# Row E of a Fourier-mixing kernel in four column tiles of TensorE, with another order of loads and weight conversions

## The chip, the cores and the metric

The kernel runs on one core of a Trainium2 chip. The metric is the device time of one execution in microseconds; the time before is the median of three runs. TensorE is PE in the profile, VectorE DVE, ScalarE ACT, GpSimd POOL, and SyncE, which here only starts transfers, SP.

## What is computed

```python
# x: (8, 3008, 256) f32; gate, val: (256, 1536); out: (1536, 256)
X = np.fft.fft(np.fft.fft(x, axis=1), axis=2).real   # (8, 3008, 256)
t = X.reshape(24064, 256)
gate = 1 / (1 + np.exp(-(t @ w_gate)))
return (gate * (t @ w_val)) @ w_out
```

The three weight matrices arrive as 64-bit floats and become 32-bit floats on the chip.

## The kernel before

Every batch is handled in two parts. First the transform along the 3008 positions: the rows of x are folded on each other by symmetry (`fold_ops`), so that 756 rows of 126 partitions times six remain, and matrices of cosines and sines (`st`, table 0 and 1) turn them into rows P (cosines), Q (sines) and E (cosines of the one feature in the middle, column `HD`), each for 1505 frequencies `k`. P and Q are 128 features wide and are named `pk` and `qk`. E is one row for each batch, but it is needed on all 128 partitions, as `ek`. Each row is made in two column blocks (even and odd frequencies, 377 and 376 columns), each block by six matmuls into two PSUM banks, `ev` and `od` (`half`); ACT copies `ev` to SBUF as `a`, and DVE places the sum and the difference of the two (`places`).

The transform along the features is merged into the weights: `merge` multiplies a piece of w_gate or w_val by the small table `dt` on PE (tile `ps`), ACT copies the result to `G1` and `G2`, and two small transfers spread one row of G2 over the partitions as `ge`, the factors of E.

The second part is the main loop. A step `i` is one half of a pair (batch, chunk of 256 frequencies, two blocks of 128 of the 1536 features). `front` makes four matmuls, `pa` from P and `pb` from Q; DVE adds E times `ge` to `pa` (`ae`, L364), and sum and difference with `pb` (`z`, L367 and L368); ACT takes the sigmoid (L575); `gate` multiplies (`h`, L379) and makes sums on POOL (`sf`). `back`, two pairs later, multiplies by the prepared forms `wf` of w_out (tile `po`). `finish` combines and stores. There are 576 steps.

Before any of it can run, the weights have to be converted, in 18 pieces, the `jobs`, each of gate (w = 0), val (1) or out (2), for column block c. `weight_load` brings one in on SP's queue, `weight_parts` is two operations on ACT (L172, L173), `weight_join` three on DVE (L182, L183, L185) and an add on POOL (L187). `weight_use` then merges a gate or val piece, or makes the forms of an out piece (POOL and ACT).

The order on every engine is the order in which the program is written (a manual schedule); waits follow from buffers. `side` and `pre` hold what is done beside a step: `at(i, f)` puts f after step i. [...] four rotate under the tag "x" (`psx`, for ps, pa, pb, ev, od), four belong to the output sums (`pso`). All transfers share eight semaphores in turn, so a transfer can wait for the one before it on its semaphore, and SP's queue waits with it.

Before, the loads start with two weight pieces, then x of batch 0, the cosines in two halves, four weight pieces, the sines in one transfer, and four more. Row E of batch 0 is made on all 128 partitions at once, with the middle column of x broadcast over 128 weight columns:

```python
W[b, blk] = (v[:, :, 0:HD], r[:, :, 0:HD],
             v[:, :, HD : HD + 1].to_broadcast([NP, NQ, P]))
```

The seven other rows E are made together in the main loop, at steps 40 and 42 (`e_rows`, seven weight columns), written to DRAM (`ed`) and read back for each batch onto 128 partitions by `seq_start`.

Of the kernel before, what the change touches and what calls it, by code (L numbers as in the profile page):

```python
# [45 lines left out]
def kernel(  # L46
# [66 lines left out]
    ge = const.tile([P, 2, NFT], F32, name="ge")  # L113

    x8 = const.tile([NP, B - 1, 4, NQ], F32, name="x8")
    ed = dram.tile([B - 1, NK], F32, name="ed")

    def load_table(t, nq):
        for q in range(0, NQ, nq):
            nc.sync.dma_start(out=st[:, t, q : q + nq], in_=stab[:, t, q : q + nq])  # L120

    jobs = [(w, c - (w == 2)) for c in range(NPR + 1) for w in range(3)
            if (c if w == 2 else c < NPR)]
    RAW, WS = {}, {}
    shared = {}
    KEEP = 10

    def weight_load(j):  # L130


        w, c = jobs[j]
        src = (moe_w_gate, moe_w_val, moe_w_out)[w]
        src = src[2 * c * P : 2 * (c + 1) * P, :] if w == 2 else src[:, c * WC : (c + 1) * WC]
        src = src.rearrange("(c p) f -> p c f", p=P)

        def some(n, pool, tag):

            key = tag, (j - 6) // 3 if tag == "c7" else 0  # L140
            if key not in shared:
                shared[key] = pool.tile([P, n, 2 * WC], F32, name=f"w{tag}", tag=tag)
            return shared[key]

        if j < KEEP:
            pool, tag = ((zp, "z"), (pqp, ("pk", "qk", "ek")[j % 3]), (op, "os"), (sp, "sf"))[
                j // 3 if j < 6 else j // 2 - 1]
            raw = pool.tile([P, 2, WC, 2], I32, name="raw", tag=tag)
            if j < 6:
                pool, tag = ((app, "ae"), (hp, "h"))[j // 3]  # L150
                ws = pool.tile([P, 2, WC], F32, name="ws", tag=tag)
            else:
                ws = some(3, cp, "c7")[:, (j - 6) % 3].rearrange("p (c f) -> p c f", c=2)
# [12 lines left out]

    def weight_parts(j):

        if j in RAW:
            raw, ws = RAW[j], WS[j]  # L170
            lo, hi = raw[:, :, :, 0], raw[:, :, :, 1]
            nc.scalar.activation(ws, hi.bitcast(F32), AF.Abs)  # L172
            nc.scalar.activation(lo, lo.bitcast(U32), AF.Copy, scale=2.0 ** -29)  # L173

    def weight_join(j):
        if j not in RAW:
            return
# [4 lines left out]
        ts(out=ws, in0=ws, scalar1=2.0 ** -15, scalar2=HUGE, op0=ALU.max, op1=ALU.min)  # L182
        ts(out=wi, in0=wi, scalar1=3, scalar2=0x3FFFFFF8, op0=ALU.logical_shift_left,  # L183
           op1=ALU.bitwise_and)
        nc.vector.scalar_tensor_tensor(out=wi, in0=hi, scalar=-(2 ** 30), in1=wi,  # L185
                                       op0=ALU.bitwise_and, op1=ALU.bitwise_or)
        nc.gpsimd.tensor_tensor(wi, wi, lo, op=ALU.add)  # L187
# [36 lines left out]
    def fold_ops(b, nq):  # L224
# [60 lines left out]
    def half(w, d, blk, sn, rows, other=None):  # L285


        c0, n = ((0, NE), (NE, NO))[blk]
        ev, od = [bank(name, other and other[i])[0:rows, 0:n] for i, name in enumerate(("ev", "od"))]

        def sums(*qs):
            for q in sorted(qs, key=lambda q: q % 2):
                mm((ev, od)[q % 2], w(q), st[:, int(sn), q, c0 : c0 + n], q < 2, q >= NQ - 2)

        def then():
            a = evp.tile([P, NE], F32, name="a", tag="a")[0:rows, 0:n]
            nc.scalar.copy(a, ev)
            return lambda: places(a)

        def places(a):  # L300
            nc.vector.tensor_tensor(d[:, blk : blk + 2 * n - 1 : 2], a, od, op=ALU.add)
            lo, hi = (od, a) if sn else (a, od)
            top = M - blk
            nc.vector.tensor_tensor(d[:, top : top - 2 * NO + 1 : -2], lo[:, 0:NO], hi[:, 0:NO],
                                    op=ALU.subtract)
        return sums, then

    def whole(sums, then):
        sums(*range(NQ))
        return then()  # L310

    def seq_start(b):
        PQE[b] = (pqp.tile([P, NK], F32, name="pk", tag="pk"),
                  pqp.tile([P, NK], F32, name="qk", tag="qk"),
                  pqp.tile([P, NK], F32, name="ek", tag="ek"))
        if b:
            nc.sync.dma_start(out=PQE[b][2], in_=ed[b - 1 : b, :].to_broadcast([P, NK]))

    def seq_group(b, blk, what, other=None):
        return half(lambda q: W[b, blk][what][:, q, :], PQE[b][what], blk, what == 1, P, other)  # L320


    ER = []

    def e_load():
        for b in range(1, B):
# [14 lines left out]
    def e_out():  # L341
        nc.scalar.dma_start(out=ed, in_=ER.pop())


    chunks = [(k0, min(CH, NK - k0)) for k0 in range(0, NK, CH)]
# [135 lines left out]


    nc.scalar.dma_start(out=dt, in_=dtab.rearrange("(c p) d -> p c d", p=P))
    for j in range(2):
        weight_load(j)
    load_x(0)
# [12 lines left out]
    weight_parts(0)  # L499
    weight_parts(1)  # L500
    weight_join(0)
    weight_join(1)
    weight_use(0)
    weight_use(1)
# [3 lines left out]
    for i, f in enumerate(fold_ops(0, NQ // 2)):  # L508
        f()
        for sums, _ in cos:  # L510
            sums(*range(i * NQ // 2, (i + 1) * NQ // 2))
    sin = [seq_group(0, blk, 1) for blk in range(2)]
    for sums, _ in sin:
        sums(*range(NQ))
# [6 lines left out]
    weight_use(2)  # L521

    per = 2 * NPR * len(chunks)
    side = {}
# [8 lines left out]


    pre = {}
    for j in range(9, len(jobs)):
        pre.setdefault(j - 9, []).append(lambda j=j: weight_parts(j))
        at(j - 9, lambda j=j: weight_join(j))
        if KEEP <= j < len(jobs) - 3:
            at(j - 9, lambda j=j: weight_load(j + 3))  # L540
# [97 lines left out]
```

## Time and profile before

| | |
|---|---|
| time, median of 3 (lowest to highest) | 2029.07 us (2028.25 to 2029.18) |
| span of the profiled execution | 2028.5 us, mean granted TensorE clock 0.996 |
| first P, E matmul / first Q matmul / first front | 23.85 / 43.84 / 54.92 us |
| last output matmul ends, by the chain | 2021.1 us |
| rows E of batches 1 to 7 | 200.63 to 204.53 and 211.21 to 215.10 us |

The page has one line for each engine with its busy time, its share of the span and its instructions. A 32-bit matmul stands in it as two records (the count of PE is twice the number of matmuls in the code), and the duration of a record is longer than the distance to the next, since matmuls overlap; the distance is what counts: 0.216 us for 256 columns, 0.317 us for 377. In a timeline each row is a start, a duration, engine and line, the operation, the result and its operand, and how many records follow each other; in square brackets is how long the engine was idle and what released it. A list of waits has the engine, its line and tile, what it waited for, the total in us, how often, and the longest.

### The profile page before, as it was taken

Reading aid. Unit: us, or ns where it says so; the run is one execution under the profiler, and the core shown is the slowest. Engines: PE = TensorE matmul, PEld = TensorE weight load, DVE = VectorE, ACT = ScalarE, POOL = GpSimd, SP = SyncE. Lnnn points to the kernel's source line nnn. Section 1 sums busy time; section 2 is a strip of 40 time slices with the busy share of each in tenths; the row PEclk is TensorE's granted clock in tenths of the full one; section 3 lists DMA queues with packets and bytes.
Section 4 is the critical chain, followed back from the end, with each engine's and each line's share of the span. In section 5 each row is a group of like instructions: output and inputs, shape, how many; then the busy total and the mean of one; then the engine's idle time right before and its main releaser. Section 6 shows DMA issues by size and latency. Waiting matters only on the chain.

```text
span 2028.5 us, 27347 instructions
## 1 busy us (share of the span) xinstructions
PE 1996.6 (98%) x9168; PEld 1743.3 (86%) x9168; DVE 1754.9 (87%) x3221; ACT 498.5 (25%) x875; POOL 1328.4 (65%) x1675
## 2 busy tenths in 40 slices
PE   5999999999999999999999999999999999999998
PEld 3788789888998889888898888988889888898888
DVE  6899778987899878997889977999879988898887
ACT  3422222222222222222222222222222222222222
POOL 3679555875569755696457955589446875565655
PEclk8999999999999999999999999999999999999999
DMA  8240002100021000200010000201002010000001
GB/s 260 84 74 11 27 11 74 33 12 11 11 81 27 11 11 17 76 26 11 16 60 28 27 16 16 73 10 37 11 11 72 16 31 11 11 16 16 11 16 26
DMA packets 136176, 70.98 MB, mean 35 GB/s; under 512 B 127875, under 2 KB 128131, under 8 KB 133642
## 3 DMA queue, kind: packets, MB, share of 16 engines
q1 hardware_dynamic: 134214, 68.69, 12.6%
q8 instruction: 74, 1.21, 0.3%
q10 hardware_dynamic: 1822, 0.54, 0.1%
q14 instruction: 66, 0.54, 0.1%
HBM read 44.50 MB, written 24.68 MB: 34 GB/s over the span
## 4 chain that ended last, share of the span: by engine, by line
PE 85%; DVE 7%; POOL 4%; DMA 2%; issue 1%; ACT 0%; DVEq 0%; SPq 0%; ACTq 0%; POOLq 0%
PE po L93 37%; PE pa L93 21%; PE pb L93 21%; PE ev L93 3%; PE od L93 3%; DVE ae L364 2%; DVE h L379 2%; DVE z L368 1%; DMA ge<-G 1%; DVE z L367 1%; POOL x L239 1%; POOL x L237 1%; DMA st<-in_stab_dram 1%; POOL sf L384 1%; POOL sf L383 1%
## 5 line engine op out<-in xcount | busy, mean ns | idle before, releaser
L575 ACT ACTIVATE z<-z 128x512 f32<-128x512 f32 (+1 forms) x576 | 358.5, 622 | 1319.1 <-DVE z L368 1319.1
L364 DVE SCALAR_TENSOR_TENSOR ae<-ek,ge,pa 128x256 f32<-128x256 f32 (+1 forms) x1152 | 489.7, 466 | 186.1 <-PE pa L93 181.9
L93 PE MATMUL pb<-qk,G 128*128 128x256 f32 (+1 forms) x2304 | 582.2, 375 | 2.5 <-DVE ae L364 2.5
L93 PE MATMUL pa<-pk,G 128*128 128x256 f32 (+1 forms) x2304 | 581.9, 375 | 0.0
L93 PE MATMUL po<-sf,wf 128*128 128x256 f32 (+1 forms) x2304 | 537.3, 376 | 1.0 <-POOL sf L384 0.2
L93 PEld LDWEIGHTS pa<-pk,G 128*128 128x128 f32 x2304 | 438.5, 190 | 55.9 <-issue 1.3
L93 PEld LDWEIGHTS po<-sf,wf 128*128 128x128 f32 x2304 | 437.2, 190 | 54.8 <-POOL sf L385 4.5
L93 PEld LDWEIGHTS pb<-qk,G 128*128 128x128 f32 x2304 | 438.2, 190 | 52.8 <-DVE ae L364 4.1
L383 POOL TENSOR_TENSOR sf<-h 128x256 f32<-128x256 f32 (+1 forms) x288 | 213.4, 741 | 386.9 <-DVE h L379 386.9
L379 DVE TENSOR_TENSOR h<-z 128x512 f32<-128x512 f32 (+1 forms) x576 | 454.7, 789 | 0.0
L367 DVE TENSOR_TENSOR z<-ae,pb 128x512 f32<-128x512 f32 (+1 forms) x576 | 390.1, 677 | 61.4 <-DVE ae L364 1.4
L93 PE MATMUL po<-h,wf 128*128 128x256 f32 (+1 forms) x1728 | 412.7, 375 | 0.0
L368 DVE TENSOR_TENSOR z<-ae,pb 128x512 f32<-128x512 f32 (+1 forms) x576 | 386.4, 671 | 0.0
L93 PEld LDWEIGHTS po<-h,wf 128*128 128x128 f32 x1728 | 329.1, 191 | 36.4
L381 POOL TENSOR_TENSOR sf<-h 128x256 f32<-128x256 f32 (+1 forms) x288 | 219.1, 761 | 210.0 <-DVE h L379 206.2
L384 POOL TENSOR_TENSOR sf<-sf,h 128x256 f32<-128x256 f32 (+1 forms) x288 | 215.4, 748 | 22.6
L385 POOL TENSOR_TENSOR sf<-h,sf 128x256 f32<-128x256 f32 (+1 forms) x288 | 214.0, 743 | 22.6
L466 ACT COPY c<-po 128x512 f32<-128x512 f32 (+1 forms) x141 | 76.7, 580 | 62.0 <-PE po L93 62.0
L93 PE MATMUL ev<-st,x 126*128 126x377 f32 (+3 forms) x216 | 78.0, 495 | 11.7 <-DMA st<-in_stab_dram 11.7
L426 DVE STREAM_TRANSPOSE os<-c 128x256 f32<-128x256 f32 x192 | 83.9, 437 | 0.2
L93 PE MATMUL od<-st,x 126*128 126x377 f32 (+3 forms) x216 | 75.3, 481 | 0.0
L471 POOL TENSOR_TENSOR c<-c 128x512 f32<-128x512 f32 (+1 forms) x47 | 73.5, 1565 | 0.0
(82 smaller groups left out, 711.4 us busy)
## 6 DMA issues: line engine op xcount, KB each, us to landing
x<-in_xf_dram SPq DMA_DIRECT2D x16, 1512.0 KB
out_dram<-os SPq DMA_DIRECT2D x288, 64.0 KB
ek<-ed SPq DMA_DIRECT2D x7, 752.5 KB
out_dram<-os SPq DMA_DIRECT2D x92, 56.0 KB
st<-in_stab_dram SPq DMA_DIRECT2D x2, 1111.9 KB
st<-in_stab_dram SPq DMA_DIRECT2D x1, 2223.7 KB
raw<-in_moe_w_gate_dram SPq DMA_DIRECT2D x4, 512.0 KB
raw<-in_moe_w_val_dram SPq DMA_DIRECT2D x4, 512.0 KB
```

Of the source, the lines that this page charges most:

```text
L93: nc.tensor.matmul(o, l, r, start=start, stop=stop, skip_group_check=True)
L364: nc.vector.scalar_tensor_tensor(out=ae[:, g], in0=ek[:, ks], scalar=ge[:, g, f : f + 1], in1=pa[:, g], op0=ALU.mult, op1=ALU.add)
L367: nc.vector.tensor_tensor(z[:, :, 0], ae, pb, op=ALU.add)
L368: nc.vector.tensor_tensor(z[:, :, 1, ::-1], ae, pb, op=ALU.subtract)
L379: nc.vector.tensor_tensor(h[:, fh], z[:, 0], z[:, 1], op=ALU.mult)
L381: tt(s[:, 2], h[:, 0, 0], h[:, 0, 1], op=ALU.subtract)
L383: tt(s[:, 0], h[:, 0, 1], h[:, 1, 1], op=ALU.add)
L384: tt(s[:, 1], s[:, 0], h[:, 0, 0], op=ALU.subtract)
L385: tt(s[:, 3], h[:, 1, 0], s[:, 1], op=ALU.subtract)
L426: nc.vector.transpose(os_[:, s, 0:nb, h, :], t[:, slot, 0 : nb * TB])
L466: nc.scalar.copy(t[:, 2 * j : 2 * j + 2, 0:n], PO[j][:, :, 0:n])
L575: nc.scalar.activation(z[:, 0], z[:, 0], AF.Sigmoid)
```

## The change

Row E of every batch is now made with one weight column for each row (one for batch 0, seven for the others). The four sums that a row needs (even or odd block, even or odd part) lie at partitions 0, 32, 64 and 96 of one PSUM bank, `pe`, that is in four column tiles of PE, and the matmuls go through the four in turn. ACT copies three of them out, DVE places the rows, and the result goes through DRAM to all partitions: for batch 0 as well, at the start, on ACT's queue. x and the cosines are loaded first, the sines in two halves, and only eight weight pieces ahead of the main loop. The conversion of the out pieces comes two pairs later in the order of the jobs, six pieces are converted ahead of the loop in place of nine, and `evacuate` has row E first. It is meant to take matmul time off PE and to let the transform start before the weights are in.

```diff
-    jobs = [(w, c - (w == 2)) for c in range(NPR + 1) for w in range(3)
-            if (c if w == 2 else c < NPR)]
+    jobs = [(w, c - 2 * (w == 2)) for c in range(NPR + 2) for w in range(3)
+            if (c >= 2 if w == 2 else c < NPR)]
-    KEEP = 10
+    KEEP = 8
...
-            W[b, blk] = (v[:, :, 0:HD], r[:, :, 0:HD],
-                         v[:, :, HD : HD + 1].to_broadcast([NP, NQ, P]))
+            W[b, blk] = (v[:, :, 0:HD], r[:, :, 0:HD], v[:, :, HD : HD + 1])
...
-    def e_rows(blk):
-        if not blk:
-            ER.append(cp.tile([B - 1, NK], F32, name="er", tag="c7"))
-        return whole(*half(lambda q: x8[:, :, 1 + 2 * blk, q], ER[0], blk, False, B - 1))
+    def e_sums(col, b, m, other=None):
+        ps = bank("pe", other)
+        tb = lambda blk, par: (2 * blk + par) * TB
+
+        def sums(*qs):
+            for n in range(max(sum(q % 2 == par for q in qs) for par in range(2))):
+                for blk in range(2):
+                    c0, k = ((0, NE), (NE, NO))[blk]
+                    for par in range(2):
+                        for q in [q for q in qs if q % 2 == par][n : n + 1]:
+                            t = tb(blk, par)
+                            mm(ps[t : t + m, 0:k], col(blk, q), st[:, 0, q, c0 : c0 + k],
+                               q < 2, q >= NQ - 2)
+
+        def then():
+            er = cp.tile([P, NK], F32, name="er", tag="c7")[0:m]
+            ev = evp.tile([P, NE], F32, name="a", tag="a")[0:m]
+            e1 = evp.tile([P, NE], F32, name="a", tag="a")[0:m]
+            nc.scalar.copy(ev, ps[tb(0, 1) : tb(0, 1) + m, 0:NE])
+            nc.scalar.copy(e1[:, 0:NO], ps[tb(1, 0) : tb(1, 0) + m, 0:NO])
+            return lambda: (places(er, 0, True, ev, ps[0:m, 0:NE]),
+                            last(er, ev, e1[:, 0:NO]))
+
+        def last(er, a, ev):
+            nc.scalar.copy(a[:, 0:NO], ps[tb(1, 1) : tb(1, 1) + m, 0:NO])
+            places(er, 1, False, ev, a[:, 0:NO])
+            nc.scalar.dma_start(out=ed[b : b + m], in_=er)
+
+    def e_spread(b):
+        (nc.sync if b else nc.scalar).dma_start(
+            out=PQE[b][2], in_=ed[b : b + 1, :].to_broadcast([P, NK]))
...
-    for j in range(2):
-        weight_load(j)
     load_x(0)
-    load_table(0, NQ // 2)
-    for j in range(2, 6):
-        weight_load(j)
-    load_table(1, NQ)
-    for j in range(6, KEEP):
+    load_table(0, 0)
+    load_table(0, NQ // 2)
+    load_table(1, 0)
+    for j in range(2):
+        weight_load(j)
+    load_table(1, NQ // 2)
+    for j in range(2, KEEP):
         weight_load(j)
...
-    cos = [seq_group(0, blk, what, (2 * blk, 2 * blk + 1) if what else None)
-           for blk in range(2) for what in (0, 2)]
+    first_e = e_sums(lambda blk, q: W[0, blk][2][:, q, :], 0, 1, 0)
+    cos = [first_e] + [seq_group(0, blk, 0) for blk in range(2)]
...
-    for then, js in zip(evacuate, ((2, 3, 4), (5,), (), (), (6, 7), (8,))):
+    for then, js in zip(evacuate, ((), (), (0,), (1, 2, 3), (4,))):
         weight_round(*js)
         then()()
+        if then is first_e[1]:
+            e_spread(0)
+    weight_round(5)
+    for j in range(3):
+        weight_use(j)
...
-    for j in range(9, len(jobs)):
-        pre.setdefault(j - 9, []).append(lambda j=j: weight_parts(j))
-        at(j - 9, lambda j=j: weight_join(j))
+    for j in range(6, len(jobs)):
+        i = j - 6 - (j > 12)
+        pre.setdefault(i, []).append(lambda j=j: weight_parts(j))
+        at(i, lambda j=j: weight_join(j))
...
-        at(2 * c + (-3, -2, 1)[w], lambda j=j: weight_use(j))
+        at((2 * c - 3, 2 * c - 2, min(2 * c + 3, j - 5))[w], lambda j=j: weight_use(j))
...
-    split(i0 + 28, e_rows, 0)
-    split(i0 + 30, e_rows, 1)
-    at(i0 + 32, e_out)
+    split(i0 + 30, lambda: whole(*e_sums(lambda blk, q: x8[:, :, 1 + 2 * blk, q], 1, B - 1)))
```

More of the change, by code (lines that the diff above doesn't have):

```diff
@@ L115, with load_table @@
     x8 = const.tile([NP, B - 1, 4, NQ], F32, name="x8")
[L116 to L120, printed above, removed]
-    jobs = [(w, c - (w == 2)) for c in range(NPR + 1) for w in range(3)
-            if (c if w == 2 else c < NPR)]
+    ed = dram.tile([B, NK], F32, name="ed")
+    def load_table(t, q):
+        nc.sync.dma_start(out=st[:, t, q : q + NQ // 2], in_=stab[:, t, q : q + NQ // 2])
+    jobs = [(w, c - 2 * (w == 2)) for c in range(NPR + 2) for w in range(3)
+            if (c >= 2 if w == 2 else c < NPR)]
     RAW, WS = {}, {}
     shared = {}
-    KEEP = 10
+    KEEP = 8
     def weight_load(j):
@@ L138, in some @@
         def some(n, pool, tag):
[L140 to L143, printed above, removed]
+            if tag not in shared:
+                shared[tag] = pool.tile([P, n, 2 * WC], F32, name=f"w{tag}", tag=tag)
+            return shared[tag]
         if j < KEEP:
-            pool, tag = ((zp, "z"), (pqp, ("pk", "qk", "ek")[j % 3]), (op, "os"), (sp, "sf"))[
-                j // 3 if j < 6 else j // 2 - 1]
+            pool, tag = ((zp, "z"), (pqp, ("pk", "qk", "ek")[j % 3]), (op, "os"))[j // 3]
             raw = pool.tile([P, 2, WC, 2], I32, name="raw", tag=tag)
@@ L152, in weight_load @@
             else:
-                ws = some(3, cp, "c7")[:, (j - 6) % 3].rearrange("p (c f) -> p c f", c=2)
+                ws = some(3, cp, "c7")[:, j - 6].rearrange("p (c f) -> p c f", c=2)
         else:
@@ L277, in fold_ops, with half @@
         for blk, (v, r) in enumerate(parts):
-            W[b, blk] = (v[:, :, 0:HD], r[:, :, 0:HD],
-                         v[:, :, HD : HD + 1].to_broadcast([NP, NQ, P]))
+            W[b, blk] = (v[:, :, 0:HD], r[:, :, 0:HD], v[:, :, HD : HD + 1])
         return ops
     PQE = {}
-    def half(w, d, blk, sn, rows, other=None):
+    def half(w, d, blk, sn):
         c0, n = ((0, NE), (NE, NO))[blk]
-        ev, od = [bank(name, other and other[i])[0:rows, 0:n] for i, name in enumerate(("ev", "od"))]
+        ev, od = bank("ev")[:, 0:n], bank("od")[:, 0:n]
         def sums(*qs):
@@ L295, in then, with places @@
         def then():
-            a = evp.tile([P, NE], F32, name="a", tag="a")[0:rows, 0:n]
+            a = evp.tile([P, NE], F32, name="a", tag="a")[:, 0:n]
             nc.scalar.copy(a, ev)
[L298 to L305, printed above, removed]
-        return sums, then
+            return lambda: places(d, blk, sn, a, od)
+        return sums, then
+    def places(d, blk, sn, ev, od):
+        nc.vector.tensor_tensor(d[:, blk : blk + 2 * ev.shape[1] - 1 : 2], ev, od, op=ALU.add)
+        lo, hi = (od, ev) if sn else (ev, od)
+        top = M - blk
+        nc.vector.tensor_tensor(d[:, top : top - 2 * NO + 1 : -2], lo[:, 0:NO], hi[:, 0:NO],
+                                op=ALU.subtract)
     def whole(sums, then):
@@ L316, in seq_start, with seq_group @@
         if b:
[L317 to L323, printed above, removed]
+            e_spread(b)
+    def seq_group(b, blk, what):
+        return half(lambda q: W[b, blk][what][:, q, :], PQE[b][what], blk, what == 1)
     def e_load():
@@ L334, in e_fold @@
         tt(x8[:, :, 3], x8[:, :, 0], x8[:, :, 2], op=ALU.subtract)
-    def e_rows(blk):
-        if not blk:
-            ER.append(cp.tile([B - 1, NK], F32, name="er", tag="c7"))
-        return whole(*half(lambda q: x8[:, :, 1 + 2 * blk, q], ER[0], blk, False, B - 1))
-    def e_out():
-        nc.scalar.dma_start(out=ed, in_=ER.pop())
+    def e_sums(col, b, m, other=None):
[22 more added lines that the diff above has]
+            nc.scalar.dma_start(out=ed[b : b + m], in_=er)
+        return sums, then
+    def e_spread(b):
+        (nc.sync if b else nc.scalar).dma_start(
+            out=PQE[b][2], in_=ed[b : b + 1, :].to_broadcast([P, NK]))
     chunks = [(k0, min(CH, NK - k0)) for k0 in range(0, NK, CH)]
@@ L483 @@
     nc.scalar.dma_start(out=dt, in_=dtab.rearrange("(c p) d -> p c d", p=P))
+    load_x(0)
+    load_table(0, 0)
+    load_table(0, NQ // 2)
+    load_table(1, 0)
     for j in range(2):
         weight_load(j)
-    load_x(0)
-    load_table(0, NQ // 2)
-    for j in range(2, 6):
-        weight_load(j)
-    load_table(1, NQ)
-    for j in range(6, KEEP):
+    load_table(1, NQ // 2)
+    for j in range(2, KEEP):
         weight_load(j)
@@ L497, in weight_round @@
             weight_join(j)
[L499 to L504, printed above, removed]
+    halves = range(NQ // 2), range(NQ // 2, NQ)
     seq_start(0)
-    cos = [seq_group(0, blk, what, (2 * blk, 2 * blk + 1) if what else None)
-           for blk in range(2) for what in (0, 2)]
-    for i, f in enumerate(fold_ops(0, NQ // 2)):
+    first_e = e_sums(lambda blk, q: W[0, blk][2][:, q, :], 0, 1, 0)
+    cos = [first_e] + [seq_group(0, blk, 0) for blk in range(2)]
+    for f, qs in zip(fold_ops(0, NQ // 2), halves):
         f()
         for sums, _ in cos:
-            sums(*range(i * NQ // 2, (i + 1) * NQ // 2))
+            sums(*qs)
     sin = [seq_group(0, blk, 1) for blk in range(2)]
-    for sums, _ in sin:
-        sums(*range(NQ))
+    for qs in halves:
+        for sums, _ in sin:
+            sums(*qs)
     evacuate = [then for _, then in cos + sin]
-    for then, js in zip(evacuate, ((2, 3, 4), (5,), (), (), (6, 7), (8,))):
+    for then, js in zip(evacuate, ((), (), (0,), (1, 2, 3), (4,))):
         weight_round(*js)
         then()()
+        if then is first_e[1]:
[3 more added lines that the diff above has]
+        weight_use(j)
     for j in range(KEEP, KEEP + 3):
         weight_load(j)
-    weight_use(2)
     per = 2 * NPR * len(chunks)
@@ L535 @@
     pre = {}
[L536 to L538 removed]
+    for j in range(6, len(jobs)):
+        i = j - 6 - (j > 12)
+        pre.setdefault(i, []).append(lambda j=j: weight_parts(j))
+        at(i, lambda j=j: weight_join(j))
         if KEEP <= j < len(jobs) - 3:
[L540 removed]
+            at(i, lambda j=j: weight_load(j + 3))
     for j in range(3, len(jobs)):
         w, c = jobs[j]
[L543 removed]
+        at((2 * c - 3, 2 * c - 2, min(2 * c + 3, j - 5))[w], lambda j=j: weight_use(j))
     i0 = 2 * NPR
```

## The prediction

> **What bounds the kernel now.** I read the page's shares first, then the waits of PE over the whole run, then the windows, and only then the chain and the timeline of the stretch that the waits point to.
>
> ```profile
> PE 1996.6 (98%) x9168; PEld 1743.3 (86%) x9168; DVE 1754.9 (87%) x3221; ACT 498.5 (25%) x875; POOL 1328.4 (65%) x1675
> ```
>
> All waits of PE, whole run (total us, times, longest):
>
> ```profile
> PE ev L93 <- DMA st<-in_stab_dram: 11.7, 2, 8.8
> PE ps L93 <- POOL ws L187: 9.3, 1, 9.3
> PE pb L93 <- DVE ae L364: 2.5, 3, 1.5
> ```
>
> Windows (stretch, then busy us and count of PE, PEld, DVE, ACT, POOL; clock, DMA share, GB/s):
>
> ```profile
> 20.00:44.00 24.00, 17.22 (x49) 10.02 (x50) 20.87 (x33) 6.94 (x12) 11.04 (x10) 0.86 0.93 266
> 55.00:100.00 45.00, 42.48 (x194) 36.21 (x193) 40.72 (x69) 24.67 (x56) 29.23 (x37) 1.00 0.31 93
> 100.00:2000.00 1900.00, 1899.04 (x8772) 1665.28 (x8771) 1657.75 (x3054) 453.47 (x784) 1266.87 (x1601) 1.00 0.11 28
> ```
>
> From 100 us on PE never rests. So there are two ways to gain: matmul time taken out of the body, and an earlier start of the dense stream. Everything before 100 us counts only by how far it moves PE. The chain in order of time says what sets the start:
>
> ```profile
> 1.25 6.31 DMA raw<-in_moe_w_val_dram
> ...
> 14.15 14.80 DMA ge<-G
> ...
> 29.38 14.32 DMA st<-in_stab_dram
> ```
>
> And the timeline of PE (start, us, then the count of records; one f32 matmul is two records):
>
> ```profile
> 23.85 2.85 PE L93 MATMUL ev<-st,x 126*128 126x377 f32 x4 [8.75 <-DMA st<-in_stab_dram]
> 43.84 3.73 PE L93 MATMUL ev<-st,x 126*128 126x377 f32 x6 [2.92 <-DMA st<-in_stab_dram]
> ...
> 54.92 1.03 PE L93 MATMUL pa<-pk,G 128*128 128x256 f32 x4
> ```
>
> The cosines land at 23.85, the sines at 43.84, and the first front (pa) starts at 54.92.
>
> [...] one weight conversion on DVE, with the POOL add of the one before it running, has L183 at 1.40 us where it takes 0.43 alone:
>
> ```profile
> 34.82 0.42 DVE L182 TENSOR_SCALAR ws<-ws 128x512 f32<-128x512 f32 x1
> 35.27 1.40 DVE L183 TENSOR_SCALAR ws<-ws 128x512 int32<-128x512 int32 x1
> 36.70 0.69 DVE L185 SCALAR_TENSOR_TENSOR ws<-raw,ws 128x512 int32<-128x512 int32 x1
> ```
>
> So a conversion costs DVE 1.5 us alone (58.17 to 59.69) and 2.5 us back to back.
>
> **The change: row E of batches 1 to 7.** Before, it stands inside the dense stream:
>
> ```profile
> 200.63 2.07 PE L93 MATMUL ev<-st,x 126*7 126x377 f32 x6
> 202.54 2.06 PE L93 MATMUL od<-st,x 126*7 126x377 f32 x6
> 204.53 1.13 PE L93 MATMUL pa<-pk,G 128*128 128x256 f32 x4
> ```
>
> That is 204.53 - 200.63 = 3.90 us, and the second half the same from 211.21: 7.8 us for 24 records, 0.317 us each. In the changed kernel the same 12 matmuls go to four column tiles in turn. The two records of one matmul use one tile and must follow each other; if starts keep program order, only the second record of one matmul can overlap the first of the next. So each matmul adds 0.317 us, not 0.634: 12 x 0.317 + 0.317 = 4.1 us[...]. Saved 7.8 - 4.4 = 3.4 us. Bounds: no overlap saves 0; all four tiles fully at once (3 x 0.634 + 0.3 = 2.2) saves 5.6. The weight loads are short (91 ns for 7 columns in this trace) and stay hidden.
>
> **The start: loads.** Two gate and value pieces (1 MB) go behind x and the cosines. At the 271 to 299 GB/s of the first 20 us that brings x and the cosines 3.7 us forward: x halves from 12.43 and 18.60 to 8.7 and 14.9, first cosines from 23.85 to 20.1; the four ge transfers of that stretch (14.80 us in the chain, while the rate fell from 299 to 247 GB/s) are gone too, so I take 19.5. Each further half table (1.1 MB) 4.4 us: 24, 28.3; two pieces at 1.3 each (ACT's conversions at 44.89 and 46.19 are paced so): 31; last half of the sines 35.2, against 43.84.
>
> **PE.** The fold needs 5.7 us from x before both column blocks are there (18.60 to 24.3 in before): 14.9 + 5.7 = 20.6, about with the table. Row E half 1, 12 records, on the half clock that a waking PE shows (0.63 each: four records from 23.85 to 26.50): 6.5 x 0.63 = 4.1, to 23.6. P half 1: 12 x 0.317 = 3.8, to 27.4. Row E half 2: 2.1, to 29.5. P half 2 to 33.3. Row E of batch 0 used to be twelve full-width matmuls, 24 records and 7.6 us at full clock; it is twelve matmuls of one weight column now, at half the path time by the same overlap.
>
> **The wait that is added.** On ACT the order is: two copies out of row E's bank, a third after DVE's first places, the row's DMA to DRAM, its spread, and only then the first copy of P. The spread waits for the row to land. From 29.5: copies 0.9, places 1.1, copy 0.5, places 0.7 gives 32.7; the row's landing was 2.1 us on idle queues (issued 222.3, spread issued 224.4), here with loads beside it 2.6: 35.3. Queued behind it: P's evacuation, hence the banks that the sine matmuls need, hence PE, idle from 33.3 to about 36.2. Still 7.6 earlier than 43.84.
>
> **DVE then sets the first front.** One pair of places is 1.0 us (40.22 to 41.13), a conversion 1.5 to 1.7 where a pair of places stands before it, so that POOL's add is over, and 2.5 where another conversion does. From 36.2 DVE has places P0 1.0, conversion 0 1.5, P1 1.0, conversion 1 1.7, 2 and 3 at 2.5, Q0 1.0, conversion 4 1.6, Q1 1.0, conversion 5 1.6: 15.4. First ae at 51.5 (55.99 before); the ge it needs, issued by ACT at about 49.1 after six conversions, land about then. PE's pa starts when Q1 is placed: 49.8. Lead at the first front 54.92 - 49.8 = 5.1 us.
>
> **What is given back.** Twelve conversions instead of nine now fall into the first steps of the main loop, where DVE takes about 5.0 us a step (59.69, 64.40, 69.64: ae 0.9, z 1.3, h 0.7, conversion 1.5 to 2.1) and PE's own work is 4.75 to 5.2. Before, PE lost 3.0 us there (pb at 70.56, 77.10 and 87.49 late by 0.97, 1.69, 0.36). After, with ae(0) 51.5, ae(3) 65.1, ae(5) 75.1: pb(4) late by 1.5, pb(5) by 0.3. Piece 10 is converted in step 4 and merged in step 5, one step later instead of three; POOL adds it 2 us after ae(5) = 77.1 (before: ae at 81.31, that step's add done at 83.2), PE is there at 73.6: 3.5 lost. Step 6 has two conversions: 1.2 lost. Sum 6.5, so 3.5 more than before. The lead shrinks to 5.1 - 3.5 = 1.6 us. Splitting the sines' load and `places` as a function cost nothing: same DVE instructions, and PE waits on ACT there.
>
> **Sum.** 1.6 + 3.4 = 5.0: 2029.07 - 5.0 = 2024.0 us.
>
> **Rivals.** (B) The tiles really overlap fourfold. [...] Against: two records per f32 matmul on one tile. Row E saves 2.2 more, and the start, where it is on the path, about 2: 2019.8, with earlier loads 2017. (C) They don't overlap at all: row E saves nothing, and the two halves at the start cost 3.5 (cold) + 1.7 more, in part hidden by the fold: about 2031, no change. For: the E matmuls of 7 columns take as long as those of 128 (0.317 each). (D) The row's round trip through DRAM waits behind the loads like ge did: 14.8 instead of 2.6 us holds ACT to 47.5, all of it on the path: 2024 + 12 = 2036, slower. For: the same queues were that slow in that stretch; against: ge are 128 single elements each, this is one row of 6 KB.
>
> **Numbers.** A (forecast) 0.45, B 0.20, C 0.21, D 0.14. The same bound is 4.06 us: faster is B and most of A (0.38), 0.58; same is C and the rest of A, 0.28; slower is D, 0.14. The range leaves out D and the best of B: 2016.5 to 2032.
>
> **What would show it.** Right: row E of batches 1 to 7 as one block of about 4.4 us near 210; first matmul near 19.5; an idle gap of PE near 33 to 36 released by ACT; first ae near 51.5; PE waits on POOL's add before ps near 74; the 300th us reached with a lead of 5. Wrong: row E's block of 2 or 7.8 us; the row's landing over 5 us; ae(0) before 48; no PE wait in the ramp.

## The result, and the profile after

The changed kernel takes 2038.8 us in the median of six runs (2037.51 to 2041.77), beside 2028.95 us for the kernel before (2027.73 to 2029.72): a ratio of 1.0051 [1.0038, 1.0064], so about 10 us slower, where 5 us faster was predicted. The profiled execution is the slowest of the six (2041.77 us, a span of 2040.0); that of the kernel before took 2030.25 us (a span of 2028.5). So the two spans stand 11.5 us apart and the two medians 9.85.

All waits of PE of over 0.2 us, whole run, after (columns as before: total us, times, longest). The line numbers are those of the changed kernel, where L184 is POOL's add at the end of a conversion, L210 a subtraction of the forms, and L293 the copy of `ev`:

```profile
PE pe L93 <- DMA st<-in_stab_dram: 20.0, 1, 20.0
PE ev L93 <- ACT a L293: 5.7, 1, 5.7
PE ps L93 <- POOL wx L184: 5.6, 2, 3.3
PE po L93 <- POOL wf L210: 3.6, 2, 3.4
PE pb L93 <- DVE ae L385: 2.3, 2, 1.5
```

Windows after, the same stretches as before:

```profile
20.00:44.00 24.00, 18.26 (x56) 8.07 (x57) 12.51 (x23) 6.74 (x13) 5.69 (x5) 0.87 0.96 313
55.00:100.00 45.00, 36.92 (x152) 30.43 (x151) 38.88 (x65) 22.13 (x48) 27.07 (x29) 0.92 0.32 95
100.00:2000.00 1900.00, 1895.39 (x8753) 1659.45 (x8752) 1656.37 (x3048) 456.71 (x792) 1270.84 (x1602) 1.00 0.11 28
```

The second line is where the time went. From 55 to 100 us PE made 194 records before and makes 152 now; it is busy for 5.6 us less, and its granted clock is 0.92 in place of 1.00. From 100 us on it is again busy nearly all the time. The chain in order of time, after:

```profile
1.64 18.23 DMA st<-in_stab_dram
20.00 3.90 PE pe L93 x12
33.06 5.08 DMA ed<-er
...
83.44 3.78 PE ps L93 x8
```

And the timeline of PE (start, duration, count of records, in brackets how long PE was idle and what released it):

```profile
20.00 3.90 PE L93 MATMUL pe<-st,x 126*1 126x377 f32 x12 [20.00 <-DMA st<-in_stab_dram]
39.13 2.88 PE L93 MATMUL ev<-st,x 126*128 126x377 f32 x4 [5.74 <-ACT a L293]
54.72 1.03 PE L93 MATMUL pa<-pk,G 128*128 128x256 f32 x4
83.44 3.78 PE L93 MATMUL ps<-wx,dt 128*128 128x256 f32 x8 [3.30 <-POOL wx L184]
98.68 3.27 PE L93 MATMUL ps<-wx,dt 128*128 128x256 f32 x8 [2.31 <-POOL wx L184]
117.04 1.22 PE L93 MATMUL po<-h,wf 128*128 128x256 f32 x2 [3.40 <-POOL wf L210]
118.06 1.91 PE L93 MATMUL pa<-pk,G 128*128 128x256 f32 x4
224.57 2.09 PE L93 MATMUL pe<-st,x 126*7 126x377 f32 x24
226.58 1.13 PE L93 MATMUL pa<-pk,G 128*128 128x256 f32 x4
```

Three things can be read here. The first matmul comes 3.85 us earlier, but the first front is where it was (54.72, before 54.92): the sines begin only at 39.13, when ACT, held by the row's way over DRAM, copies P out. Then PE stops three times for POOL, at steps 5, 7 and 10 (83.44, 98.68 and 117.04), and works more slowly after each stop: four records of `pa` take 1.91 us instead of 1.03, eight of `ps` 3.78 instead of 1.97. And row E of batches 1 to 7 is a single block from 224.57 to 226.58: 2.0 us, before 7.8.

The sum fits the spans. Step 16 begins at 119.81 before and at 137.28 after, 17.5 us later; what comes after it is shorter by the row's 6.0 (from step 24 to step 100 the trace shows 264.8 us before and 258.8 after); 17.5 - 6.0 = 11.5, the difference of the spans. In every version below that has the tiles for batches 1 to 7, the span is the start of step 16 plus 1902.1 to 1902.7 us (1904.2 in the last one, whose row takes 1.9 us longer), in the kernel before plus 1908.7. So each version can be judged by two numbers of its trace: when DVE makes the first `ae`, and how long it takes from there to step 16.

### The profile page after: what moved, and what is told of

Read it like the earlier page. It is cut to its first block, busy times and chain, and to the rows that moved or that the text cites. A ratio compares the mean times of both kernels' runs of the same rounds, so it can differ in the third digit from the quotient of the medians.

```text
span 2040.0 us, 27352 instructions
## 1 busy us (share of the span) xinstructions
PE 1994.4 (98%) x9168; PEld 1737.8 (85%) x9168; DVE 1755.3 (86%) x3221; ACT 499.6 (24%) x877; POOL 1332.5 (65%) x1675
## 4 chain that ended last, share of the span: by engine, by line
PE 85%; DVE 8%; POOL 4%; DMA 1%; issue 1%; ACT 0%; DVEq 0%; SPq 0%; ACTq 0%; POOLq 0%
PE po L93 37%; PE pa L93 21%; PE pb L93 20%; PE ev L93 3%; PE od L93 3%; DVE ae L385 2%; DVE h L400 2%; DVE z L389 2%; DVE z L388 1%; POOL x L236 1%; DMA st<-in_stab_dram 1%; POOL x L234 1%; POOL sf L405 1%; POOL sf L404 0%; DVE os L447 0%
## 5 line engine op out<-in xcount | busy, mean ns | idle before, releaser
L93 PE MATMUL ev<-st,x 126*128 126x377 f32 (+1 forms) x192 | 69.2, 493 | 5.7 <-ACT a L293 5.7
L226 POOL TENSOR_TENSOR x<-x 126x510 f32<-126x510 f32 (+1 forms) x43 | 62.2, 1445 | 15.1 <-DMA x<-in_xf_dram 15.1
```

What stands on the lines that cost most here:

```text
L93: nc.tensor.matmul(o, l, r, start=start, stop=stop, skip_group_check=True)
```

## The experiments

Theory 1: the tiles gain 6 us; the loss lies in the first twelve steps, where a piece is converted only one step before it is needed, so that PE waits and its clock falls. Rivals: the row's landing on ACT is the whole loss (rival 1); DVE's sum of work sets the pace whatever the order (rival 2); the loads lose by themselves (rival 3).

### Row E of batches 1 to 7 alone

The kernel before, with this as its only edit (`e_sums` as in the change, but with its own `ed` of seven rows):

```diff
-    split(i0 + 28, e_rows, 0)
-    split(i0 + 30, e_rows, 1)
-    at(i0 + 32, e_out)
+    split(i0 + 30, lambda: whole(*e_sums(lambda blk, q: x8[:, :, 1 + 2 * blk, q], 1, B - 1)))
```

> The kernel before with one part of the change: row E of batches 1 to 7 is computed in four column tiles at step i0+30 in place of its two wide groups. Loads, conversions and batch 0 stay as before. Theory 1 (the 24 records of the tiles overlap fully and the block falls from 7.8 to 2.0 us; the loss of the whole change lies in its first twelve loop steps): 2029.0 - 5.8 = about 2023.2 us, between 2022 and 2025, and pa of step 0 still near 54.9 us. Rival (what the row saves is taken back by another wait near 220 us, because an engine other than TensorE sets the pace there): 2027 to 2029.

Measured: 2024.07 us, ratio 0.9969 [0.9956, 0.9981], as theory 1 said. Once more, on another chip:

> The version that takes from the change only row E in tiles for batches 1 to 7, once more, so that it stands on one chip beside the other candidates: 2022 to 2026 us, 0.9969 of the kernel before as the first time; if the first run was favoured by its chip, 0.998 or more.

2022.57 us, 0.9972 [0.9961, 0.9982]. The loop's gain came twice and is 6 us, and this part of the change alone is faster than both kernels. The first front shows how far a single start can move: 57.86 us in the first profile, 52.46 in the second, with the sines landing at 45.48 and at 43.06. From the first `ae` to step 16 it is 63.8 us in both, as in the kernel before. So below, starts of single profiles are compared with care, and stretches within a profile freely.

### The row's landing, moved out of ACT's way

```diff
         then()()
-        if then is first_e[1]:
-            e_spread(0)
+    e_spread(0)
     weight_round(5)
```

> The changed kernel, with the transfer that reads row E of batch 0 back from DRAM issued by ACT after all evacuations instead of in the middle of them. Theory 1 (the row's landing costs the lead at the first front, and the larger loss comes later, where PE waits for POOL): the sines begin near 33 to 34 us instead of 39.1, pa of step 0 comes 3 to 5 us earlier, and the waits in the first twelve steps stay or grow, since conversions and not the start set their end: 2034 to 2038 us. Rival 1 (the landing of the row on ACT is the whole loss): the loss goes and the saving at row E shows, 2023 to 2025 us.

Measured: 2033.59 us, ratio 1.0018 [1.0011, 1.0025], just under theory 1's range and 8.6 us over rival 1's. Three of PE's waits in this version:

```profile
PE ps L93 <- POOL wx L184: 6.5, 2, 3.3
PE po L93 <- POOL wf L210: 3.9, 2, 3.6
PE ev L93 <- ACT a L293: 0.8, 1, 0.8
```

The wait for ACT falls from 5.7 to 0.8 us, the sines begin at 34.43, `pa` of step 0 at 48.81 (5.9 earlier), and the time falls by 0.0033 of 2029, some 6.7 us. The waits for POOL are as long as ever. So the landing is one loss, about 6 us, and not the whole: more than that still stands between this version and the tiles alone.

### Row E of batch 0 wide again

The broadcast weights and the two wide groups of the kernel before for batch 0, in the order of the changed kernel:

```diff
-    first_e = e_sums(lambda blk, q: W[0, blk][2][:, q, :], 0, 1, 0)
-    cos = [first_e] + [seq_group(0, blk, 0) for blk in range(2)]
+    cos = [seq_group(0, blk, what, (2 * blk, 2 * blk + 1) if what else None)
+           for blk in range(2) for what in (2, 0)]
```

> The changed kernel with row E of batch 0 computed wide again (128 equal rows, as the kernel before does it) and so without its way over DRAM; loads first, late conversions and the tiles for batches 1 to 7 stay. Theory 1 (the late conversions set the end of the first twelve steps): the sines no longer wait for the row, but six wide groups are summed and evacuated instead of four and a row; pa of step 0 lands within 3 us of 54.7, the waits on POOL at steps 5, 7 and 10 stay, 2035 to 2041 us. Rival 1 (the way over DRAM is the whole loss): 2023 to 2029 us.

Measured: 2034.31 us, ratio 1.0022 [1.0013, 1.0031], a little under theory 1's lower end; PE waits 11.3 us for POOL, as expected. `pa` of step 0 stands at 48.57, 6 us earlier than in the changed kernel, where it had been expected within 3 us of it. This is the same place as with the late transfer (48.81): tiles for batch 0 save matmul time that nobody waits for at that point, while DVE sets the first `ae` (50.31 and 50.57). PE is busy without a gap from 20 to 48.6 us here, but shortening that only makes it wait for DVE.

### Filling the stalls

Five matmuls of 256 columns on data that is ready, in three places, in `merge` ahead of its own matmuls and ahead of `back`; their sums are overwritten or not read:

```diff
+        if (g, c) in ((0, 4), (0, 5)):
+            fill(ps)
...
+        if i == 10:
+            fill(bank("ps"))
```

> The changed kernel with three groups of five extra matmuls of 256 columns (about 2.3 us each, their sums overwritten or unread) placed where PE waits for POOL: ahead of the merges of the pieces that step 5 and step 7 take, and ahead of the out matmuls of step 10. Theory 1 (about 7.7 of the 17.5 us lost by step 16 is matmuls at half granted clock, which follow the three stalls): the granted clock stays at 1.0 between 84 and 130 us, and the time falls by 4 to 8 us, to 2031 to 2035 us. Rival 2 (the chain of conversions on DVE and POOL sets the pace of these steps, so that a faster PE only waits longer at the same places): 2037 to 2040 us. If the granted clock falls for a reason other than the stalls, it still falls, and the time grows by up to 7 us, the extra matmuls.

Measured: 2037.15 us, ratio 1.0033 [1.002, 1.0045], so 3.7 us under the changed kernel (the two intervals overlap a little), in spite of 7 us of extra matmuls. That lies in rival 2's range and not in theory 1's. Windows of PE to POOL and the clock, with the fill:

```profile
84.00:100.00 16.00, 14.98 (x69) 12.67 (x69) 14.71 (x24) 8.17 (x19) 10.33 (x11) 1.00 0.45 133
100.00:120.00 20.00, 16.52 (x76) 13.91 (x75) 17.97 (x30) 6.52 (x15) 15.43 (x19) 1.00 0.11 28
```

and without it, in the changed kernel:

```profile
84.00:100.00 16.00, 13.69 (x50) 11.24 (x49) 13.01 (x21) 6.35 (x14) 9.55 (x10) 0.82 0.36 101
100.00:120.00 20.00, 16.37 (x62) 13.33 (x61) 16.43 (x27) 7.70 (x18) 14.96 (x20) 0.84 0.18 53
```

The clock stays at 1.00, so it was the stalls that lowered it. From the first `ae` to step 16 it is 77.3 us instead of 81.4 (a second profile of the same first steps, that of the last experiment, has 81.5). But the waits for POOL do not go: with the fills, PE still waits 6.2 us for it. A faster PE waits longer for the same conversions. Theory 1 holds for the cause of the low clock, but only about 4 us belong to it; the rest looks here as rival 2 has it.

### How far ahead: eight pieces, nine pieces

First eight pieces ahead of the loop, and later ones in step j-8:

```diff
-    weight_round(5)
+    weight_round(5, 6, 7)
...
-    for j in range(6, len(jobs)):
-        i = j - 6 - (j > 12)
+    for j in range(8, len(jobs)):
+        i = j - 8
```

> The changed kernel with eight pieces converted ahead of the loop instead of six, and each later piece j converted in step j-8 (before: j-6 or j-7). Theory 1, now said more closely (DVE is busy without a gap in the first nine steps, where it converts one piece of about 2 us per step beside its share of the front; each piece moved into the loop puts the conversion one step nearer to its merge, until PE waits for it and its clock is halved): two pieces more ahead put the first ae 4 to 5 us later, to about 60 us, but the waits for POOL at steps 5, 7 and 10 shrink to under 1 us each, the granted clock stays at 1.0, and step 16 begins 4 to 9 us earlier than 137.3: 2030 to 2035 us. Rival (how far ahead the conversions run doesn't matter, DVE has the same work either way and only its sum counts): the later first front takes back what the waits give, 2037 to 2041 us.

Measured: 2040.94 us, ratio 1.0056 [1.0043, 1.0068], in the rival's range: theory 1 failed here. Three of its waits:

```profile
PE po L93 <- POOL wf L210: 8.7, 4, 3.6
PE pb L93 <- DVE ae L385: 5.3, 4, 3.0
PE ps L93 <- DVE z L389: 0.7, 2, 0.4
```

The merges no longer wait for POOL at all, as expected; in their place PE waits 8.7 us for the forms. Those of the out pieces c = 2 to 4 are still made in step 2c+3, and the out matmuls of step 2c+4 read them. There are two slacks, from conversion to merge and from forms to out matmuls, and the change shortened both. The same with row E of batch 0 wide:

> Both repairs at once: row E of batch 0 wide, without its way over DRAM, and eight pieces converted ahead; loads of x and cosines first and tiles for batches 1 to 7 stay. Theory 1 (the two losses are separate: some 6 us at the first front, the rest in the steps after it): first ae near 55 us, no wait for POOL of over 1 us, 2021 to 2028 us, so faster than the kernel before. Rival (an earlier front only makes PE wait longer for the same conversions): as with the six ahead, 2033 to 2036 us.

2036.92 us, ratio 1.0036 [1.0024, 1.0049], so the expected 2021 to 2028 failed too: with 8.8 us of waits for the forms, an earlier first `ae` (55.01) is worth about 4 us, and the version is no faster than with six ahead. Then the second slack:

```diff
-        at((2 * c - 3, 2 * c - 2, min(2 * c + 3, j - 5))[w], lambda j=j: weight_use(j))
+        at((2 * c - 3, 2 * c - 2, max(2 * c + 1, j - 7))[w], lambda j=j: weight_use(j))
```

> The changed kernel with eight pieces converted ahead, as in e_ahead8, and the forms of the out pieces made as early as the conversion allows: in step max(2c+1, j-7) instead of min(2c+3, j-5), so two or three steps before the out matmuls that read them instead of one. e_ahead8 took away the waits at the merges (5.6 to 0.7 us) and got 8.7 us of waits for the forms in their place. Theory 2 (two slacks were shortened, conversion to merge and conversion to forms, and either alone stalls PE): the waits of po on POOL fall under 1 us, the granted clock stays at 1.0 after 70 us, step 16 begins at 125 to 129 instead of 137: 2028 to 2033 us. Rival (DVE's sum of work sets the pace and any wait that is removed comes back elsewhere): 2037 to 2042 us.

2034.08 us, ratio 1.0024 [1.0014, 1.0035]: the waits for the forms fall from 8.7 to 3.2 us, one wait, at step 10, which had been expected under 1; step 16 begins at 127.45, 9.8 earlier than in the changed kernel. By the ratios the time is 5.5 us under that kernel's, and the median stands 1 us above the expected range. The one wait that is left is for the one piece (c = 3) whose forms are made two steps before they are read, in step 8 for step 10; all others now have three steps, and none of them is waited for. With row E of batch 0 wide:

> The same two edits (eight ahead, forms as early as they can be) on the version with row E of batch 0 wide and so without its way over DRAM; loads of x and cosines first and tiles for batches 1 to 7 stay. Theory 2: as wide8 (2036.9 us), less its 8.8 us of waits for the forms and the half clock after them: 2021 to 2027 us, and so near or below the version that takes from the change only row E in tiles for batches 1 to 7. Rival (DVE's sum of work): 2034 to 2038 us.

2032.3 us, ratio 1.0013 [1.0006, 1.002], between the two expectations, so that of 2021 to 2027 failed. The same wait of 3.2 us at step 10 is left, and `pb` waits 7.8 us for DVE's `ae`. Eight ahead is not enough. Nine, with the whole schedule of the kernel before, on the changed kernel (row E of batch 0 put together in a part of G2 that is still free):

```diff
-    jobs = [(w, c - 2 * (w == 2)) for c in range(NPR + 2) for w in range(3)
-            if (c >= 2 if w == 2 else c < NPR)]
+    jobs = [(w, c - (w == 2)) for c in range(NPR + 1) for w in range(3)
+            if (c if w == 2 else c < NPR)]
...
-    KEEP = 8
+    KEEP = 10
...
-    weight_round(5)
+    weight_round(5, 6, 7, 8)
...
-    for j in range(6, len(jobs)):
-        i = j - 6 - (j > 12)
+    for j in range(9, len(jobs)):
+        i = j - 9
...
-        at((2 * c - 3, 2 * c - 2, min(2 * c + 3, j - 5))[w], lambda j=j: weight_use(j))
+        at(2 * c + (-3, -2, 1)[w], lambda j=j: weight_use(j))
```

> The changed kernel with the conversion schedule of the kernel before: nine pieces ahead of the loop, piece j in step j-9, and the out pieces in their old places; loads of x and cosines first and row E in tiles for all batches stay (row E of batch 0 is put together in a part of G2 that is still free, since the buffers c7 are taken by pieces). Theory 1: first ae 6 to 7 us later, near 62 us, no wait for POOL of over 1 us in the first twelve steps, granted clock 1.0, step 16 near 127 us: 2026 to 2031 us. Rival (only the sum of DVE's work counts): 2037 to 2041 us.

2030.18 us, ratio 1.0006 [0.9997, 1.0014], 9 us under the changed kernel and in theory 1's range. This is the test that decides against rival 2, which had said 2037 to 2041: DVE has the same conversions to make in both versions, only three of them stand ahead of the first `ae` and not behind it. PE's waits after the first front, but for two of 0.5 and 0.4 us on ACT and DVE:

```profile
PE pb L93 <- DVE ae L387: 6.6, 4, 3.9
PE po L93 <- POOL sf L407: 0.2, 1, 0.2
```

No wait for a conversion or a form is left. Finally the load order, with nine ahead and row E of batch 0 wide, so that only the loads, the place of the first two conversions and the tiles for batches 1 to 7 differ from the kernel before:

> The kernel before with only two parts of the change: row E of batches 1 to 7 in tiles, and x and cosines loaded first (the conversions of the first two pieces, which then land later, stand after the first row sums). Nine pieces ahead and all other places as before. It tells what the load order alone is worth, beside the version with the tiles alone (2024.1 us). Theory 2: PE ends the row sums near 48 us, but DVE, with nine conversions behind the sums, gives the first ae only near 57 us, a little later than before's 56.0; no wait for POOL in the loop; 2022 to 2027 us, within 3 us of the tiles alone. Rival (the load order is a gain or a loss of its own): below 2020 or above 2029 us.

2026.71 us, ratio 0.9991 [0.9983, 1.0]: in the expected range, but about 4 us slower than the tiles alone on the same chip, where 3 had been the most expected. For this part rival 3 is right. The first front of PE comes at 49.00, but the first `ae` at 58.21: the first two conversions, which DVE did before while it waited for x, now stand behind the row sums.

The two numbers of each version, from its trace (us), and the ratio:

| version | first `ae` | from there to step 16 | ratio |
|---|---|---|---|
| before | 55.99 | 63.8 | 1 |
| tiles for 1 to 7 alone (twice) | 58.93, 53.53 | 63.8, 63.8 | 0.9969, 0.9972 |
| and x first, nine ahead (wide9) | 58.21 | 63.9 | 0.9991 |
| and row of batch 0 over DRAM, nine ahead (e_sched) | 61.55 | 63.9 | 1.0006 |
| x first, six ahead, row of batch 0 wide (e_wide0) | 50.31 | 78.9 | 1.0022 |
| changed, row's transfer late (spread_late) | 50.57 | 79.0 | 1.0018 |
| changed, stalls filled (e_fill) | 55.91 | 77.3 | 1.0033 |
| changed, eight ahead / forms early too | 60.32 / 59.04 | 76.6 / 68.4 | 1.0056 / 1.0024 |
| row wide, eight ahead / forms early too | 55.01 / 56.69 | 75.1 / 71.5 | 1.0036 / 1.0013 |
| changed | 55.85 | 81.4 | 1.0051 |

The loss can be read as a chain of versions that differ in one main part each: the tiles alone stand at 0.9972, x first adds about 3.9 us (wide9), the way of row E of batch 0 over DRAM 3.0 (e_sched), and the conversions nearer to their use 9.1 (changed). The price of the way over DRAM is not fixed: with six ahead it was 6 us, with eight 4 and 2.

With nine ahead the stretch is 63.8 or 63.9 us in five profiles, whatever the start. With six it is 77 to 81. The three conversions moved into the loop are some 2 us of DVE each (piece 10's, in step 4 of the changed kernel, runs from 79.14 to 81.56). DVE's busy time in the stretch is the third figure of each line, before and changed:

```profile
55.99:119.81 63.82, 61.30 (x280) 52.67 (x279) 59.47 (x102) 28.93 (x66) 44.35 (x59) 1.00 0.28 85
55.85:137.28 81.43, 69.68 (x281) 57.55 (x279) 68.35 (x115) 33.94 (x73) 52.33 (x65) 0.90 0.26 79
```

So 8.9 of the 17.6 us are DVE at work, and 8.7 are time in which DVE, too, waits: it is idle for 13.1 us in place of 4.4. The trace of the changed kernel shows that part as a circle, first DVE:

```profile
80.46 1.10 DVE L182 SCALAR_TENSOR_TENSOR wx<-wx 128x512 int32<-128x512 int32 x1
...
88.97 0.87 DVE L385 SCALAR_TENSOR_TENSOR ae<-ek,ge,pa 128x256 f32<-128x256 f32 x2 [2.58 <-PE pa L93]
```

then POOL:

```profile
82.11 1.28 POOL L184 TENSOR_TENSOR wx<-wx 128x512 int32<-128x512 int32 x1
```

DVE ends the conversion of piece 10 at 81.56, behind `ae` and `z` of step 4 and `h` of step 3; POOL adds at 82.11, behind three sums of `gate`; PE merges at 83.44, and only after that comes `pa` of step 6 (87.02). DVE, which had fallen behind, now waits 2.58 us for that `pa` before `ae` of step 6 at 88.97, and behind this `ae` stand the next two conversions, for which PE waits in turn at step 7. With a piece converted one step before its merge the three engines take turns. More distance cuts this circle: with nine ahead a piece is converted two or three steps before its merge and the forms are made three steps before they are read, and no such version shows such a wait.

### The order of the tiles

```diff
-            for n in range(max(sum(q % 2 == par for q in qs) for par in range(2))):
-                for blk in range(2):
...
-                    for par in range(2):
-                        for q in [q for q in qs if q % 2 == par][n : n + 1]:
+            for blk in range(2):
...
+                for par in range(2):
+                    if True:
+                        for q in [q for q in qs if q % 2 == par]:
```

> The changed kernel with the matmuls of row E in another order: all six records of one column tile, then those of the next, instead of tile after tile in turn. Theory A (the tiles overlap only where neighbours in program order go to different tiles): only neighbours at the seams overlap, and the block of batches 1 to 7 near 220 us takes 6 to 8 us instead of 2.0. Theory B [...]: 2.0 us as before.

A single execution took 2042.61 us. The block in this version:

```profile
223.90 4.01 PE L93 MATMUL pe<-st,x 126*7 126x377 f32 x24
227.84 1.13 PE L93 MATMUL pa<-pk,G 128*128 128x256 f32 x4
```

3.9 us from its start to the next `pa`: neither 2.0 nor 6 to 8. In the changed kernel, where the matmuls go through the tiles in turn, the first records of the block start at (ns from its first):

```
in turn:       0 7 14 20 | 325 332 337 344 | 642 649 655 662 | 961 ...
```

Four records start within 20 ns, the next four 0.32 us later, and so on in six groups of four. The program has, in each round, the four records of 377 columns (two matmuls of two records) ahead of the four of 376. Yet the two that start at 14 and 20 are of 376, and the next two of 377 start only at 325 and 332. So the starts of these records did not keep the program's order. Both theories missed the 3.9 us; what sets them was not shown.

## Why the prediction was wrong

**Row E of batches 1 to 7.** "If starts keep program order" failed. The saving was predicted at 3.4 us, with a bound of 5.6, and is 6.0: the prediction had the right case as its rival B. That order was an assumption of the author, and the record starts above (two records of 376 columns at 14 and 20 ns, two of 377 that stand ahead of them at 325 and 332) show the opposite for these 32-bit matmuls. The predicted 4.4 us, and the 2.2 of the bound, have in them 0.3 us beyond the matmuls themselves, a guess of the author's that no run shows: six records in a row at 0.317 are 1.9 of the block's 2.01 us.

**Loads and the sums.** Predicted and measured: x halves 8.7 and 14.9 (9.32 and 15.50), first cosines 19.5 (20.00), P done 33.3 (39.13 - 5.74 = 33.39). The loads were right; that the sums ended so near is in part luck: row E was reckoned from 19.5 although the fold was to end at 20.6 (it began at 20.00, with the column block that was ready); the second half of row E took 1.4 us (27.96 to 29.34) and not 2.1, since the tiles ran together (four records start within 20 ns); and the first half of P took 4.1 and not 3.8.

**The wait that is added.** The place was right, ACT's queue behind the row's landing; the size was off: "here with loads beside it 2.6" measured 5.08. The sines began at 39.13 instead of 36.2. It is rival D's mechanism at a smaller size, and moving it out of the way gave 6.7 us.

**The first front.** "15.4" us of DVE measured 16.7 (39.13 to 55.85), so the first `ae` came at 55.85 rather than 51.5, and the lead of 5.1 us was 0.2. DVE itself was ready at 55.35 and waited 0.49 us for `pa`: after the stall of 5.74 us PE took 6.0 us (39.13 to 45.11, at a granted clock of 0.54) for ten records that take 3.2 at full clock, which the prediction had not counted.

**What is given back.** This is the step that decided the result: 3.5 us were predicted, and from step 0 to step 16 the changed kernel takes 17.7 us more (82.6 against 64.9). The first wait was seen rightly, with its size: piece 10, 3.5 predicted, 3.30 measured; and the waits of `pb` in steps 4 and 5, 1.5 and 0.3 predicted, were 0.83 and 1.46. But the sum stopped at step 6, with DVE's time, and three terms were too small or missing: the wait of step 7 was put at 1.2 and is 2.31; the forms, which the change also moved to one step before their use, cost 3.40 at step 10 and were never asked about; and the clock falls at the stalls (0.50 for 6.83, 3.41 and 6.83 us), which the prediction counted for the first matmuls only. PE waits 11.7 us in these steps against 2.5 before, 9.2 more. Of the other 8.5 some 7.7 are matmuls at half clock, by the distances of their starts, though the fill shows that only about 4 of them would have been saved by a full clock, since PE waits again at the next piece.

**The sum.** Predicted -5.0. Row E is better by 2.6, the lead worse by 4.9, the ramp worse by 14.2: -5.0 - 2.6 + 4.9 + 14.2 = +11.5, the difference of the two spans. By the medians it is 9.85, so some 1.7 us of these terms belong to the two executions that were profiled. The range reached to 2032 and left out D; the result lies beyond D too, because the ramp was taken as one number in all cases, with no bound of its own.

Why wide8_forms, with an earlier first `ae` than ahead8_forms, took 3.1 us more on the way to step 16 can be read in the traces. DVE's `ae` of step 6 waited 2.37 us for the landing of its factors `ge`, in place of 0.65; and after nearly the same stall at step 10 (3.17 and 3.18 us) step 11 took 5.14 us in place of 3.45, its four records of `pa` 1.85 in place of 1.03 (granted clock from 100 to 120 us 0.91, in place of 1.00). The trace of ahead8_forms is that of its fastest execution (2031.52 us, median 2034.08), so this need not be a difference of the versions. What stays open: why that `ge` landed later, and which of the 3.2 us at step 10 with eight ahead is DVE's and which POOL's. In ahead8_forms POOL waits 2.54 us for DVE's `h` and then works without a gap from 103.90 to 110.42, with the forms last.

## What to carry to other kernels

When work is moved closer to its use, count for each piece how many steps lie between its making and its reading, for every reader, and ask whether the reader stands ahead of what the maker needs next: at a distance of one step the engines went round in a circle, at two the forms were still late by 3.2 us, and at three they were not. A gain at the start is worth only what the next engine can take up; here PE's first front was free to move by 6 us while DVE's first `ae` decided. And a part of a change that gains inside the dense stretch should be tried alone: the tiles for batches 1 to 7 gave 6 us, and everything put beside them took more than that.

## What was not expected of the hardware

The 32-bit matmuls of four column tiles ran at once: 24 records of 376 and 377 columns, seven weight columns each, in 2.0 us instead of 7.8, four of them starting within 20 ns; in another order of the same matmuls, 3.9.

The clock fell at stalls of 2.31 to 3.40 us. In the changed kernel it was granted at 0.50 from 82.17 to 89.00, from 99.24 to 102.65 and from 116.31 to 123.13 us, at stalls of 3.30, 2.31 and 3.40 us that end at 83.44, 98.68 and 117.04, and at 1.00 between these stretches; through the stall of 1.46 that ends at 77.28 it stayed at 1.00. The version with the late transfer has `ps` at full speed after a stall of 3.29 (eight records in 1.99 us) and at half after one of 3.26 (3.78); the version with row E of batch 0 wide keeps full speed after one of 2.40 (1.99); in the filled version, with waits of up to 2.23, the clock was 1.00 from 84 to 300 us. So the length of a stall alone does not tell in these runs whether the clock falls; what else decides was not shown.

One row of 5.9 KB, written to DRAM while the loads ran at 290 GB/s (33 to 38.2 us), took 5.08 us from issue to landing, where seven rows in the kernel before, with 20 GB/s moved (222.3 to 224.4 us), had taken 2.1 until their spread was issued.
